# First x halves as two 128-row tiles each, and w1's first slices on another queue, in a SiLU MLP with gradients

## The chip, the cores and the metric

The kernel runs on one core of a Trainium2 chip. The metric is device time in microseconds (us) of one execution; lower is better. Five engines work side by side, each on its own instruction stream: TensorE (PE, with weight loads shown as PEld), VectorE (DVE), ScalarE (ACT), GpSimd (POOL) and SyncE (SP), which here only issues transfers. Transfers issued by SP or ACT wait in that engine's queue and are carried out by DMA engines.

## The reference

A two-layer MLP without bias, and all its gradients. S = 2048 rows, D = 640, F = 1536, everything bf16.

```python
def _fwd_reference(x, w1, w2):
    h = jnp.einsum("bsd,df->bsf", x, w1)
    h = _silu(h)
    out = jnp.einsum("bsf,fd->bsd", h, w2)
    return out

def reference(x, w1, w2, grad_out):
    _out, _vjp = jax.vjp(_f, x, w1, w2)
    _grads = _vjp(grad_out)
    return (_out, *_grads)
```

So there are four outputs: out, and the gradients of x, w1 and w2. In matrix terms: h = x w1, a = silu(h), out = a w2; g = grad_out w2^T, gh = g * silu'(h); gx = gh w1^T, gw1 = x^T gh, gw2 = a^T grad_out.

## The kernel before, in words

The rows are taken in four chunks of SC = 512 (the loop over c, L284). Everything in a chunk is held transposed: features on the 128 partitions, 512 rows along the free axis. D is five blocks of 128 (index dt), F is twelve (index ft), and w1 is loaded in three column thirds of FC = 512 (index fc).

For each chunk there are four matmul stages: h (L206, five matmuls per ft), out (sd_phase, L269, with w2), g (L253) and gx (sd_phase again, with w1T). ScalarE turns h into a (silu_a, L215) and into a tanh (L219); VectorE makes the derivative from it (L221, L222). Two more stages behind the loop compute gw2 (L357) and gw1 (L406, L387) over all rows.

The change is at the very start, before and in the first chunk:

- **Warm matmuls.** L140 to L145: VectorE fills a tile `warm`, and TensorE runs NWARM = 22 matmuls 128x128x128 on it. Nothing reads their result.
- **First loads.** The first chunk's x is not loaded by a transposing transfer, as the later ones are (load_xT, L157), but as it lies in memory, in two halves of 256 rows (load_x_half, L171) into `x_two`. Partition p of a half holds the two adjacent rows 2p and 2p+1, so one partition's data is one run of 2560 bytes. Then come slices of the first column third of w1 (load_w1_rows, L177): row block 0, row block 1, and row blocks 2 to 4. Then the second and third column third (load_w1, L168), w2 (L186), and transposing loads of grad_out, w2 and w1 (L187 to L190). All of these are issued by SP, in this order.
- **Start before the entry wait.** All engines meet at a barrier at the start of the program. The instructions gathered in the list `early` (and whatever precedes them on the same engine) are moved ahead of an engine's wait at that barrier by start_before_entry_wait (L16): the memset, the warm matmuls, both x halves and the first two w1 slices. The third slice and all that follows on SP comes after the wait.
- **ScalarE's first work.** After the barrier: the load of its function table and one activation on a single column (L185), so that the table is there when it is needed.
- **PE transposes.** pe_x_half (L192) takes a half: for each of the five dt, two 128x128 transposes on TensorE (L197, through the identity `ident` that GpSimd makes) into one PSUM tile `tp`, then one copy PSUM to SBUF into `xT` (L199), by VectorE for even dt and ScalarE for odd dt. As a tile holds every second row of the half, the copy writes with a step of two elements (the rearrange "p (s q) -> p q s").
- **First h stage.** h_first (L232) runs the first KM = 2 row blocks dt for the four ft of the first column third in turn (dt outside, ft inside; four PSUM banks open), then for each of these ft the rest of dt, and then ft 4 to 11 whole. So the w1 slices are needed one after the other: block 0 by the first four matmuls, block 1 by the next four, blocks 2 to 4 from the ninth on; the second column third from the twenty-first.

PSUM has eight tiles in the pool ps_h (tag "hp"), shared by the transposes and all matmul groups. What an engine does, and in what order, is the order written in the program after the tile scheduler has arranged it; semaphore waits are added by the framework.

Of the kernel before, what the change touches and what calls it, by code (L numbers as in the profile page):

```python
# [9 lines left out]
ACT = mybir.ActivationFunctionType  # L10
# [5 lines left out]
def start_before_entry_wait(nc, names):  # L16

    def move(nc):
        blocks = nc.m.functions[0].blocks
        entry, home = blocks[0].instructions, blocks[1].instructions
        for engine in {i.engine for i in home if i.name in names}:
            mine = [i for i in home if i.engine == engine]
            last = max(k for k, i in enumerate(mine) if i.name in names)
            moved = mine[: last + 1]
            gate = next(
                k
                for k, i in enumerate(entry)  # L30
                if i.engine == engine and isinstance(i, mybir.InstEventSemaphore)
            )
            taken = {i.name for i in moved}
            for k in reversed(range(len(home))):
                if home[k].name in taken:
                    del home[k]
            for i in reversed(moved):
                entry.insert(gate, i)

    nc.at_finalize(move)  # L40
# [22 lines left out]
def kernel(  # L63
# [11 lines left out]
    nc = tc.nc  # L75
    P = 128
    x2 = x.flatten_outer_dims()
# [5 lines left out]
    S, D = x2.shape  # L83
    F = w1.shape[1]
    ST, DT, FT = S // P, D // P, F // P
    SC = 512
    NCH = S // SC
    STC = SC // P
    FC = 512
# [1 line left out]
    FB = FC // P  # L91
    LAG = 2
    LAG_G = 4
    KM = 2
    NWARM = 22
    dt_in = x.dtype

    dram = ctx.enter_context(tc.tile_pool(name="dram", bufs=1, space=bass.MemoryType.DRAM))
# [13 lines left out]
    w1_v = w1.rearrange("(dt p) f -> p dt f", p=P)  # L112
    w2_v = w2.rearrange("(ft p) d -> p ft d", p=P)
    x_v = x2.rearrange("(st p) d -> p st d", p=P)
# [17 lines left out]
    with ExitStack() as mctx:  # L132
        cpool = mctx.enter_context(tc.tile_pool(name="cpool", bufs=1))
# [6 lines left out]
        warm = cpool.tile([P, P], dt_in, name="warm")  # L140
        early = [nc.vector.memset(warm[:], 1.0)]
        warm_a = cpool.tile([P, 1], FP32, name="warm_a")
        wp = ps_h.tile([P, SC], FP32, name="wp", tag="hp")
        for i in range(NWARM):
            early.append(nc.tensor.matmul(wp[:, 0:P], lhsT=warm[:], rhs=warm[:], start=True, stop=True))  # L145

        ident = cpool.tile([P, P], dt_in, name="ident")
        make_identity(nc, ident[:])

        w1_nat = w1pool.tile([P, DT, F], dt_in, name="w1_nat", tag="w1a")  # L150
# [12 lines left out]
            return goT  # L163

        xT_next = xpool.tile([P, DT, SC], dt_in, name="xT")
        x_two = cpool.tile([P, 2, 2, D], dt_in, name="x_two")

        def load_w1(lo, hi):  # L168
            nc.sync.dma_start(out=w1_nat[:, :, lo:hi], in_=w1_v[:, :, lo:hi])

        def load_x_half(half):  # L171
            lo = half * 2 * P
            return nc.sync.dma_start(
                out=x_two[:, half, :, :], in_=x2[lo:lo + 2 * P, :].rearrange("(p q) d -> p q d", q=2)
            )

        def load_w1_rows(lo, hi):  # L177
            return nc.sync.dma_start(out=w1_nat[:, lo:hi, 0:FC], in_=w1_v[:, lo:hi, 0:FC])

        early += [load_x_half(0), load_x_half(1), load_w1_rows(0, 1), load_w1_rows(1, KM)]  # L180
        load_w1_rows(KM, DT)
        start_before_entry_wait(nc, {i.ins.name for i in early})
        for fc in range(1, NFC):
            load_w1(fc * FC, (fc + 1) * FC)
        nc.scalar.activation(warm_a[:], warm[:, 0:1], ACT.Silu)  # L185
        nc.sync.dma_start(out=w2_nat[:], in_=w2_v[:])  # L186
        goT_next = load_goT(0)  # L187
        for fc in range(NFC):
# [1 line left out]
        nc.sync.dma_start_transpose(out=w1T[:], in_=w1[:, :])  # L190

        def pe_x_half(xT, half):  # L192
            lo = half * 2 * P
            for dt_ in range(DT):
                tp = ps_h.tile([P, 2, P], dt_in, name="tp", tag="hp")
                for q in range(2):
                    nc.tensor.transpose(tp[:, q, :], x_two[:, half, q, dt_ * P:(dt_ + 1) * P], ident[:])  # L197
                copy = nc.scalar.copy if dt_ % 2 else nc.vector.tensor_copy
                copy(out=xT[:, dt_, lo:lo + 2 * P].rearrange("p (s q) -> p q s", q=2), in_=tp[:])  # L199

        pe_x_half(xT_next, 0)
        pe_x_half(xT_next, 1)

        def h_mm(hp, ft, xT, lo, hi):
            for dt_ in range(lo, hi):
                nc.tensor.matmul(  # L206
                    hp[:],
                    lhsT=w1_nat[:, dt_, ft * P:(ft + 1) * P],
                    rhs=xT[:, dt_, :],
                    start=(dt_ == 0),  # L210
                    stop=(dt_ == DT - 1),
                )
# [19 lines left out]
        def h_first(xT, aT, ghT):  # L232
            hps = []
            for ft in range(FB):
                hps.append(ps_h.tile([P, SC], FP32, name="hp"))
            for dt_ in range(KM):
                for ft in range(FB):
                    h_mm(hps[ft], ft, xT, dt_, dt_ + 1)
            for i in range(FT + LAG_G):
                if i < FT:  # L240
                    if i < FB:
                        h_mm(hps[i], i, xT, KM, DT)
                    else:
# [40 lines left out]
        for c in range(NCH):  # L284
            xT, goT = xT_next, goT_next
# [13 lines left out]
            if c == 0:  # L299
                h_first(xT, aT, ghT)  # L300
                nc.sync.dma_start(
                    out=aT_scr[:, c * SC:(c + 1) * SC].rearrange("(ft p) s -> p ft s", p=P), in_=aT[:]
                )
                sd_phase(c, w2_nat, aT, oT_scr)
                for ft in range(FT):
                    g_group(ft, goT, ghT)
                nc.sync.dma_start(
                    out=ghT_scr[:, c * SC:(c + 1) * SC].rearrange("(ft p) s -> p ft s", p=P), in_=ghT[:]
# [4 lines left out]
            for i in range(FT + LAG):  # L313
# [7 lines left out]
                out=aT_scr[:, c * SC:(c + 1) * SC].rearrange("(ft p) s -> p ft s", p=P), in_=aT[:]  # L321
            )
            nc.sync.dma_start(
                out=ghT_scr[:, c * SC:(c + 1) * SC].rearrange("(ft p) s -> p ft s", p=P), in_=ghT[:]
# [7 lines left out]
    with ExitStack() as fctx:  # L332
# [45 lines left out]
        for fc in range(NFC):  # L378
            gh_blk = gh_blks[fc]
            for dt_ in range(DT):  # L380
                if dt_ == DT // 2:
                    store_gw2(fc)
                if fc == NFC - 1 and dt_ == DT - 1:
                    for k, (lo, hi) in enumerate(((0, FC - P), (FC - P, FC))):
# [12 lines left out]
                        else:  # L397
                            nc.vector.tensor_copy(out=g1[:, lo:hi], in_=gp[:, lo:hi])  # L398
                        last_store = nc.sync.dma_start(
                            out=gw1_v[:, dt_, fc * FC + lo:fc * FC + hi], in_=g1[:, lo:hi]  # L400
# [49 lines left out]
```

## Time and profile before

| | us |
|---|---|
| median of 8 runs | 321.0 |
| lowest and highest of these | 320.64, 321.67 |
| the profiled execution: time | 321.24 |
| the profiled execution: span in the profile | 319.5 |
| HBM read and written | 9.83 MB, 28.97 MB |

The profile shows one execution. Its span (319.5) starts with the program's first instruction; the rest of that execution's time (1.74) lies around it. "Busy" of TensorE counts matmuls in flight; since they are pipelined, the distance from start to start tells the rate, and the length of a single one does not. In a timeline, `x20` means that twenty instructions in a row are put in one line, from the first one's start to the last one's end; the brackets tell how long the engine was idle before and what ended that. In the chain that ended last each line is a piece of work that the next one waited for, or followed on its engine. A DMA's issue and its landing are different times: "to landing" is the time from the issue to the last semaphore signal. w1_nat and w2_nat both appear as `w_nat`, since the profile leaves digits out of names.

### The profile page before, as it was taken

What the parts mean: (1) busy time and instruction counts of PE and PEld (TensorE: products, weight loads), DVE (VectorE), ACT (ScalarE), POOL (GpSimd) and SP (SyncE); (2) the same over time, 40 slices, a digit from 0 to 9 for tenths busy, and PEclk for the clock granted to TensorE, in tenths of its full rate; (3) what the DMA queues carried; (4) which work ended last, traced back from release to release, by engine and by line L of the source; (5) the groups of instructions that cost most, each with busy time, mean ns of one, the idle gap of its engine ahead of it and who ended that gap; (6) DMA issues with size and microseconds to landing.
All of it is one profiled execution on the core that took longest, in us unless ns stands there. A gap on an engine that the chain in (4) does not pass through costs nothing.

```text
span 319.5 us, 3570 instructions
## 1 busy us (share of the span) xinstructions
PE 316.2 (99%) x1498; PEld 146.3 (46%) x1498; DVE 102.6 (32%) x182; ACT 77.9 (24%) x142; POOL 0.7 (0%) x6
## 2 busy tenths in 40 slices
PE   9999999999999999999999999999999999999996
PEld 6444444444444444444444444444444444444443
DVE  3771541477510087710147741000000100001001
ACT  4960000545201254411054520110100001001100
POOL 0000000000000000000000000000000000000000
PEclk9999999999999999999999999999999999999999
DMA  8999999999999855292635079809999998995111
GB/s 284 306 197 223 237 307 245 336 261 295 284 275 280 223 187 143 85 309 76 170 109 139 2 258 267 217 23 297 261 215 270 264 261 286 239 292 176 50 37 45
DMA packets 147311, 67.33 MB, mean 211 GB/s; under 512 B 112608, under 2 KB 147040, under 8 KB 147296
## 3 DMA queue, kind: packets, MB, share of 16 engines
q1 hardware_dynamic: 147296, 67.12, 80.9%
q8 instruction: 11, 0.18, 0.2%
q14 instruction: 4, 0.03, 0.0%
HBM read 9.83 MB, written 28.97 MB: 121 GB/s over the span
## 4 chain that ended last, share of the span: by engine, by line
PE 98%; DMA 1%; DVE 0%; issue 0%; DVEq 0%; SPq 0%
PE hp L269 32%; PE hp L206 16%; PE hp L357 16%; PE hp L253 16%; PE hp L406 15%; PE hp L387 1%; DMA x_two<-in_x_dram 1%; PE tp L197 1%; DVE g L398 0%; DVEq L398 0%; SPq L434 0%
## 5 line engine op out<-in xcount | busy, mean ns | idle before, releaser
L206 PE MATMUL hp<-xT,w_nat 128*128 128x512 bf16 x240 | 57.4, 381 | 0.0
L253 PE MATMUL hp<-goT,w2T 128*128 128x512 bf16 x240 | 56.9, 379 | 0.0
L269 PE MATMUL hp<-aT,w_nat 128*128 128x512 bf16 x240 | 52.5, 379 | 0.0
L269 PE MATMUL hp<-ghT,w1T 128*128 128x512 bf16 x240 | 52.5, 379 | 0.0
L357 PE MATMUL hp<-a_blk,go_nat 128*128 128x512 bf16 x240 | 52.0, 379 | 0.0
L406 PE MATMUL hp<-gh_blk,x_nat 128*128 128x512 bf16 x224 | 48.5, 379 | 0.0
L277 ACT ACTIVATE oT<-hp 128x512 bf16<-128x512 f32 x24 | 14.3, 597 | 109.8 <-PE hp L269 109.8
L215 ACT ACTIVATE aT<-hp 128x512 bf16<-128x512 f32 x48 | 29.9, 625 | 33.0 <-PE hp L206 33.0
L206 PEld LDWEIGHTS <-w_nat 128*128 128x128 bf16 x240 | 23.7, 99 | 28.4 <-issue 0.7
L269 PEld LDWEIGHTS <-w1T 128*128 128x128 bf16 x240 | 23.5, 98 | 28.3
L253 PEld LDWEIGHTS <-w2T 128*128 128x128 bf16 x240 | 23.5, 98 | 28.3
L357 PEld LDWEIGHTS <-go_nat 128*128 128x128 bf16 x240 | 23.5, 98 | 28.3
L269 PEld LDWEIGHTS <-w_nat 128*128 128x128 bf16 x240 | 23.4, 97 | 28.4
L279 DVE CAST oT<-hp 128x512 bf16<-128x512 f32 x16 | 11.1, 692 | 76.9 <-PE hp L269 76.9
L260 DVE SCALAR_TENSOR_TENSOR ghT<-ghT,hp 128x512 bf16<-128x512 bf16 x48 | 32.5, 682 | 7.3 <-PE hp L253 7.3
L406 PEld LDWEIGHTS <-x_nat 128*128 128x128 bf16 x224 | 21.9, 98 | 26.4
L222 DVE SCALAR_TENSOR_TENSOR ghT<-aT,v 128x512 bf16<-128x512 bf16 x48 | 32.8, 688 | 0.5
L221 DVE TENSOR_SCALAR v<-t 128x512 bf16<-128x512 f32 x48 | 20.3, 426 | 30.5 <-ACT t L219 30.5
L219 ACT ACTIVATE t<-hp 128x512 f32<-128x512 f32 x48 | 29.8, 625 | 0.0
L417 DVE CAST g<-hp 128x512 bf16<-128x512 f32 x7 | 4.8, 692 | 47.1 <-PE hp L406 27.4
L367 DVE CAST g2T<-hp 128x512 bf16<-128x512 f32 x7 | 4.8, 692 | 46.1 <-PE hp L357 46.1
L365 ACT ACTIVATE g2T<-hp 128x512 bf16<-128x512 f32 x8 | 4.8, 597 | 47.0 <-PE hp L357 47.0
(20 smaller groups left out, 27.0 us busy)
## 6 DMA issues: line engine op xcount, KB each, us to landing
aT_scr<-aT SPq DMA_DIRECT2D x4, 1536.0 KB, 6.2
ghT_scr<-ghT SPq DMA_DIRECT2D x4, 1536.0 KB, 8.0
out_dram<-o_sb SPq DMA_DIRECT2D x8, 640.0 KB, 3.6
oT_scr<-oT SPq DMA_DIRECT2D x4, 640.0 KB, 3.6
go_nat<-in_grad_out_dram SPq DMA_DIRECT2D x4, 640.0 KB, 6.6
x_nat<-in_x_dram SPq DMA_DIRECT2D x4, 640.0 KB, 5.3
gxT_scr<-oT SPq DMA_DIRECT2D x4, 640.0 KB, 4.7
w_nat<-in_w_dram SPq DMA_DIRECT2D x1, 1920.0 KB, 12.9
```

The costliest lines, as they stand in the source:

```text
L206: nc.tensor.matmul(hp[:], lhsT=w1_nat[:, dt_, ft * P:(ft + 1) * P], rhs=xT[:, dt_, :], start=(dt_ == 0), stop=(dt_ == DT - 1),)
L215: nc.scalar.activation(aT[:, ft, :], hp[:], ACT.Silu)
L219: nc.scalar.activation(t[:], hp[:], ACT.Tanh, scale=0.5)
L221: nc.vector.tensor_scalar(out=v[:], in0=t[:], scalar1=-0.5, scalar2=0.5, op0=ALU.mult, op1=ALU.add)
L222: nc.vector.scalar_tensor_tensor(out=ghT[:, ft, :], in0=aT[:, ft, :], scalar=1.0, in1=v[:], op0=ALU.subtract, op1=ALU.mult)
L253: nc.tensor.matmul(gp[:], lhsT=w2T[:, dt_, ft * P:(ft + 1) * P], rhs=goT[:, dt_, :], start=(dt_ == 0), stop=(dt_ == DT - 1),)
L260: nc.vector.scalar_tensor_tensor(out=ghT[:, ft, :], in0=ghT[:, ft, :], scalar=1.0, in1=gp[:], op0=ALU.add, op1=ALU.mult)
L269: nc.tensor.matmul(op_[:], lhsT=w_all[:, ft, dt_ * P:(dt_ + 1) * P], rhs=rhs_all[:, ft, :], start=(ft == 0), stop=(ft == FT - 1),)
L277: nc.scalar.activation(oT[:, dt_, :], op_[:], ACT.Copy)
L279: nc.vector.tensor_copy(out=oT[:, dt_, :], in_=op_[:])
L357: nc.tensor.matmul(gp[:], lhsT=go_nat[:, st, dt_ * P:(dt_ + 1) * P], rhs=a_blk[:, st, :], start=(st == 0), stop=(st == ST - 1),)
L406: nc.tensor.matmul(gp[:], lhsT=x_nat[:, st, dt_ * P:(dt_ + 1) * P], rhs=gh_blk[:, st, :], start=(st == 0), stop=(st == ST - 1),)
```

## The change

Four things are altered, all at the start:

1. x halves: each half is loaded as two tiles of 128 consecutive rows (`x_first`, through the view x_v), so partition p holds rows p and 128 + p of the half, two runs of 1280 bytes. The transposes read these tiles, and the copy writes 256 adjacent elements. KT = DT, so all five column blocks are loaded and copied.
2. w1's three slices are issued by ScalarE instead of SP, and are now row block 0, row block 1, and row blocks 2 to 4, all three in `early`. The activation on `warm_a` stands ahead of them in the text and is, by its place on that engine, moved ahead of the entry wait with them. In the built program ScalarE's order is: slice of block 0, table load, activation, slice of block 1, slice of blocks 2 to 4, entry wait. SP's is: both x halves, entry wait, the second and third column third of w1, w2, and then the transposing loads.
3. KM is 3 instead of 2.
4. NWARM is 23 instead of 22.

Later in SP's order a few transfers change places (for instance the transposing load of the third chunk's x now comes ahead of the first store of oT).

```diff
-    KM = 2
-    NWARM = 22
+    KM = 3
+    NWARM = 23
+    KT = DT
...
-        x_two = cpool.tile([P, 2, 2, D], dt_in, name="x_two")
+        x_first = cpool.tile([P, STC, KT * P], dt_in, name="x_first")
...
         def load_x_half(half):
-            lo = half * 2 * P
-            return nc.sync.dma_start(
-                out=x_two[:, half, :, :], in_=x2[lo:lo + 2 * P, :].rearrange("(p q) d -> p q d", q=2)
-            )
+            rows = slice(2 * half, 2 * half + 2)
+            return nc.sync.dma_start(out=x_first[:, rows, :], in_=x_v[:, rows, 0:KT * P])
 
         def load_w1_rows(lo, hi):
-            return nc.sync.dma_start(out=w1_nat[:, lo:hi, 0:FC], in_=w1_v[:, lo:hi, 0:FC])
-
-        early += [load_x_half(0), load_x_half(1), load_w1_rows(0, 1), load_w1_rows(1, KM)]
-        load_w1_rows(KM, DT)
+            return nc.scalar.dma_start(out=w1_nat[:, lo:hi, 0:FC], in_=w1_v[:, lo:hi, 0:FC])
+
+        early += [load_x_half(0), load_x_half(1)]
+        nc.scalar.activation(warm_a[:], warm[:, 0:1], ACT.Silu)
+        early += [load_w1_rows(0, 1), load_w1_rows(1, 2), load_w1_rows(2, DT)]
         start_before_entry_wait(nc, {i.ins.name for i in early})
         for fc in range(1, NFC):
             load_w1(fc * FC, (fc + 1) * FC)
-        nc.scalar.activation(warm_a[:], warm[:, 0:1], ACT.Silu)
         nc.sync.dma_start(out=w2_nat[:], in_=w2_v[:])
...
         def pe_x_half(xT, half):
-            lo = half * 2 * P
-            for dt_ in range(DT):
+            for dt_ in range(KT):
                 tp = ps_h.tile([P, 2, P], dt_in, name="tp", tag="hp")
                 for q in range(2):
-                    nc.tensor.transpose(tp[:, q, :], x_two[:, half, q, dt_ * P:(dt_ + 1) * P], ident[:])
+                    nc.tensor.transpose(tp[:, q, :], x_first[:, 2 * half + q, dt_ * P:(dt_ + 1) * P], ident[:])
                 copy = nc.scalar.copy if dt_ % 2 else nc.vector.tensor_copy
-                copy(out=xT[:, dt_, lo:lo + 2 * P].rearrange("p (s q) -> p q s", q=2), in_=tp[:])
+                copy(out=xT[:, dt_, half * 2 * P:(half + 1) * 2 * P], in_=tp[:])
```

## The prediction

> **What bounds the kernel now.** I read the busy shares first, then the chain that ended last, then the first 20 us of the timeline, then the DMA issues.
>
> ```profile
> PE 316.2 (99%) x1498; PEld 146.3 (46%) x1498; DVE 102.6 (32%) x182; ACT 77.9 (24%) x142; POOL 0.7 (0%) x6
> ```
>
> TensorE is busy for all but 3.3 us of the span, so only the start and the end can give or cost anything. The chain in order of time (start, length, what):
>
> ```profile
> 0.09 3.05 DMA x_two<-in_x_dram
> 3.18 2.31 PE tp L197 x20
> 5.49 13.42 PE hp L206 x60
> 18.91 12.95 PE hp L269 x60
> ```
>
> The chain is: the first x half lands at 3.14, twenty transposes follow, then sixty h matmuls. Sixty matmuls of the same shape take 13.42 us here and 12.95 in the next stage (0.216 each), so the first sixty lose 0.47 us. The weight loads show where:
>
> ```profile
> 5.18 0.26 PEld L206 LDWEIGHTS <-w_nat 128*128 128x128 bf16 x2
> 5.71 0.15 PEld L206 LDWEIGHTS <-w_nat 128*128 128x128 bf16 x1 [0.28 <-issue]
> 6.14 0.15 PEld L206 LDWEIGHTS <-w_nat 128*128 128x128 bf16 x1 [0.28 <-issue]
> 6.45 2.47 PEld L206 LDWEIGHTS <-w_nat 128*128 128x128 bf16 x12 [0.16 <-issue]
> ```
>
> The first matmuls start at 5.29, 5.71, 6.14 and 6.45: steps of 0.42, 0.43 and 0.31, then 0.216. Nothing is waited for ("issue"): TensorE runs at half rate and changes to full rate inside the third step, at 6.14 + 0.43 x (0.31 - 0.216)/(0.43 - 0.216) = 6.33. The same doubling shows in the 128-column shape:
>
> ```profile
> 0.50 2.53 PE L145 MATMUL wp<-warm 128*128 128x128 bf16 x22 [0.50 <-DVE warm L141]
> 315.80 0.67 PE L387 MATMUL hp<-gh_blk,x_nat 128*128 128x128 bf16 x9
> ```
>
> Less one matmul's own length (0.31 and 0.22), these are 21 steps of 0.106 and 8 of 0.056. The granted clock stands at 1.00 in both windows, so it does not show this. Two consequences: a delay before 6.33 costs half (the work put off is done at twice the rate), a delay behind it costs all.
>
> The data arrive thus (us from issue to landing):
>
> ```profile
> w_nat<-in_w_dram SPq DMA_DIRECT2D x2, 640.0 KB, 7.5
> x_two<-in_x_dram SPq DMA_DIRECT2D x2, 320.0 KB, 3.2
> w_nat<-in_w_dram SPq DMA_DIRECT2D x1, 384.0 KB, 4.2
> w_nat<-in_w_dram SPq DMA_DIRECT2D x2, 128.0 KB, 3.5
> ```
>
> With the issue times on SP's queue (0.09 and 0.54; 1.00, 1.48, 2.05; 2.48) and the single values (3.0 and 3.4 for x; 6.9 for the first 640 KB alone): x half 0 at 3.14, half 1 at 3.97, w1 row block 0 at 4.4, block 1 at 5.1, blocks 2 to 4 at 6.2, the second column third at 9.34. All stand in one queue, in the order in which TensorE reads them.
>
> **The change part by part.**
>
> *Warm matmuls, 22 to 23.* One more step of 0.106 moves their end from 2.82 to 2.93. It lies in the wait for x (until 3.18), which is 0.36 long: nothing. Were x there by 2.93, it would cost up to 0.1.
>
> *Contiguous copies.* Ten copies (DVE 445 ns, ACT 447 ns each) may get shorter. The fourth DVE copy, which the first h matmul needs, runs from 4.81 to 5.24, and the last transpose holds TensorE until 5.29. So they are hidden behind half-rate transposes: nothing. If the rate doubled before the transposes were done, the copy would be last; half of a copy, 0.2 us, bounds the gain.
>
> *KM = 3.* The same 60 matmuls in another order. Bank 0 is complete after 14 instead of 11, so ScalarE's Silu stream starts 3 x 0.216 = 0.65 later. Its last aT now ends at 19.75 (18.95 + 0.80), and its reader is the twelfth matmul of the next stage, 18.75 + 11 x 0.216 = 21.1. The cover is 1.37 us, of which 0.72 is left: nothing. Without cover TensorE would wait for the rest.
>
> *x as two 128-row tiles.* 640 KB now come in runs of 1280 B instead of 2560 B. The bandwidth row of the first 30 us, one figure for each 0.75 us,
>
> ```profile
> GB/s 0 65 280 393 357 257 362 365 369 351 358 355 357 367 361 360 364 367 344 212 42 96 291 301 13 46 279 290 287 111 173 229 290 142 144 211 290 193 108 227
> ```
>
> shows 393 GB/s while the long runs move (its fourth figure) and about 360 while 1 to 1.3 KB runs do: 0.655 MB takes 1.82 instead of 1.67 us, so half 0 is 0.07 and half 1 0.15 later.
>
> *w1's slices on ScalarE's queue.* The changed program's order there is: slice of block 0, table load (1.28), warm activation (0.20), slice of block 1, slice of blocks 2 to 4. ScalarE is ready at 0.14, so with 0.43 per issue they leave at about 0.14, 2.1 and 2.55, done by 2.95; its first copy is at 3.82, so the issuing is hidden (0.87 us of cover). SP loses three issues, and the second and third column thirds of w1 (640 KB each) and w2 leave some 1.4 us sooner, at about 1.0, 1.5 and 2.1. These are now in flight **beside** the slices instead of behind them. Two prices follow.
>
> First, block 0 (131 KB, 0.36 us at 360 GB/s) competes with x. If it goes wholly ahead of the rest of half 0, that lands at 3.57, and the twenty transposes (2.13 at 0.106) end at 5.74, 0.45 late. If it delays half 1 alone, that lands at 4.48, and its ten transposes end at 5.59, 0.30 late; with block 1 ahead as well, 0.66 late. If nothing goes ahead, half 1 at 4.12 is in time for its turn at 4.25: nothing. At half price that is 0 to 0.35; I take 0.2.
>
> Second, blocks 2 to 4 are needed by the ninth h matmul (7.53 now, 7.73 after the first price). Now 1.31 MB have moved when they land at 6.2; when the second column third lands at 9.34, 1.97 MB have. The lower end is 6.2, nothing lost. The upper end is that the whole 640 KB goes ahead: 9.34, 1.6 lost at full price. Equal shares let some 0.34 MB ahead, that is 1.65 MB, by interpolation 7.8. I take 1.75 MB, nearer to equal shares than to the far end: 6.2 + 0.44/0.655 x 3.14 = 8.3, so 0.55 lost. Behind it the ACT stream and everything else are late by the same.
>
> [...] No row here shows two queues at once.
>
> *The other loads.* The second column third has the same 1.97 MB to move up to its end, so it lands as before (9.34, first read at 10.1). w2 lands at 3.58 + 12.9 = 16.5, read at 18.75. A few later stores and transposing loads on SP change places, but from 6.45 on TensorE steps at 0.216 with no wait to the end: nothing.
>
> **Sum.** 0.2 + 0.55 = 0.75. The profiled execution took 321.24, of which the span is 319.5; it would take 321.99. It stands 0.24 above the median of the runs, so against the median of 321.0 the forecast is **321.7 us**, slower by 0.2%.
>
> **Rivals.**
>
> *No late slice (not slower).* The queues share so that blocks 2 to 4 land by 7.7; then only the first price is left, 321.0 + 0.2 = 321.2, or 321.0 if block 0 too goes by unnoticed. For it: 1.5 us of slack now (6.2 against 7.53). Against it: 1.3 MB beside it that used to stand behind it. It turns on the landing of one transfer: at 7.7 it is free, each 0.1 later costs 0.1.
>
> *The rate doubles later.* TensorE's pause before the transposes grows from 0.36 to as much as 0.6 us. If the rise comes a fixed time after the pause (3.15 after 3.18), x's delay costs double, 0.2 more: 321.9. If it makes the whole run-up from 0.50 to 6.33 begin anew at the end of the pause, at about 3.6, full rate comes at 9.4, 3.1 late, at half price 1.5: 323.2 with the first price alone. Against it: the pause of 0.36 did not prevent the rise at 6.33.
>
> [...]
>
> *Faster.* If the rate usually doubles before the transposes end, the shorter copies show (0.2); if x also lands no later and the 0.47 of half-rate loss goes too, 321.0 - 0.2 - 0.47 = 320.3. Against it: the transfers of x got shorter runs and company.
>
> **How the numbers follow.** No change means within 0.2%, 0.64 us: about what runs that spread over 1.03 us can tell. Forecast 0.44, its own range 321.3 to 322.8, of which 0.08 lies within 0.2%; no late slice 0.34, all within; rate later 0.14, slower; faster 0.08. So slower 0.36 + 0.14 = 0.50, same 0.08 + 0.34 = 0.42, faster 0.08. The range for 8 in 10 goes from 320.7, where the first rival and the lowest of the runs shown lie together, to 322.8 (0.2 and the 1.6 of the far end); the last two rivals' far ends are left out.
>
> **What would show it.** The slices of block 1 and of blocks 2 to 4 land after 5.1 and 6.2, and TensorE has a wait on w_nat before the ninth h matmul; x half 1 lands after 4.25 and the transposes end after 5.29; copies under 445 ns without effect. I am wrong if the h matmuls step at 0.216 from the rise on without a gap (then 321.0 to 321.2), or if half-rate steps last beyond 7 us (then above 322).

## The result and the profile after

The changed kernel takes 323.2 us (median of 11 runs, 322.34 to 323.61); the kernel before, timed beside it, 320.8 (31 runs, 320.43 to 322.26). The ratio is 1.0067, 95% interval 1.0057 to 1.0077: slower by 2.2 us (the ratio is of means; the medians differ by 2.4). The forecast was slower, 321.7, with a range up to 322.8; the time lies above the range.

The profiled execution took 323.29 with a span of 320.7, against 319.5 before. The spans of the eleven runs go from 320.3 to 321.7 with a median of 321.2, so this profile shows a quick one. It shows 1.3 us of the loss, all of it in the first 8.2 us: from 7.98 on TensorE works at the same step as before, and the first h stage ends at 20.23 instead of 18.91. The chain that ended last in the kernel after (start, length, what), which answers to the chain shown of before:

```profile
0.08 3.84 DMA x_first<-in_x_dram
...
3.97 1.25 PE tp L195 x10
5.21 0.04 issue
5.26 1.25 PE tp L195 x10
6.50 13.73 PE hp L204 x60
```

The first half of x lands at 3.92 instead of 3.14, the second half makes TensorE wait once more, and the transposes end 1.0 later. The sixty h matmuls take 13.73 where they took 13.42. The weight loads show why:

```profile
3.96 0.98 PEld L195 LDWEIGHTS <-x_first 128*128 128x128 bf16 x10 [1.09 <-DMA x_first<-in_x_dram]
5.25 0.98 PEld L195 LDWEIGHTS <-x_first 128*128 128x128 bf16 x10 [0.31 <-DMA x_first<-in_x_dram]
6.19 0.26 PEld L204 LDWEIGHTS <-w_nat 128*128 128x128 bf16 x2
6.72 0.15 PEld L204 LDWEIGHTS <-w_nat 128*128 128x128 bf16 x1 [0.28 <-issue]
7.15 0.15 PEld L204 LDWEIGHTS <-w_nat 128*128 128x128 bf16 x1 [0.28 <-issue]
7.58 0.15 PEld L204 LDWEIGHTS <-w_nat 128*128 128x128 bf16 x1 [0.28 <-issue]
7.98 2.04 PEld L204 LDWEIGHTS <-w_nat 128*128 128x128 bf16 x10 [0.25 <-issue]
```

The pause before the transposes grew from 0.4 to about 1.1 us, and a second one of 0.3 follows. Four h matmuls (from 6.30, 6.72, 7.15 and 7.58) run at half rate, where it was two and a part. By the prediction's formula the rate doubles at 7.58 + 0.43 x (0.40 - 0.216)/(0.43 - 0.216) = 7.95 instead of 6.33. So x is later and the full rate is later too.

The timeline of ScalarE and its queue, and the DMA issues of the first 30 us, show what x had beside it:

```profile
0.20 0.40 ACTq L177 DMA_DIRECT2D w_nat<-in_w_dram  x1
0.65 1.28 ACT L180 ACT_TABLE_LOAD   x1 [0.65 <-POOLq L432]
0.71 0.88 ACTq L177 DMA_DIRECT2D w_nat<-in_w_dram  x2
...
1.94 0.20 ACT L180 ACTIVATE warm_a<-warm 128x1 f32<-128x1 bf16 x1
```

```profile
x_first<-in_x_dram SPq DMA_DIRECT2D x2, 320.0 KB, 4.2
w_nat<-in_w_dram ACTq DMA_DIRECT2D x1, 384.0 KB, 7.1
w_nat<-in_w_dram ACTq DMA_DIRECT2D x2, 128.0 KB, 3.9
```

The slices did not stay behind the table load. The issuing of the second and third (0.71 to 1.59) runs while the table load (0.65 to 1.93) is under way, though both stand behind the activation in the order. So all three slices leave by 1.6. Block 0 lands at 3.74, x's half 0 at 3.92, block 1 at 5.01, x's half 1 at 5.21. Before, the same 896 KB landed in the order half 0 (3.14), half 1 (3.97), block 0 (4.4), block 1 (5.12). The last of them lands at about the same time; what is needed first now comes last. In the window from 2 to 3 us the two queues (q1 is SP's, q10 ScalarE's; packets, MB, share) are both at work, with 164 and 129 packets:

```profile
q1 hardware_dynamic: 164, 0.20, 56.6%
q10 hardware_dynamic: 129, 0.12, 45.2%
```

### The profile page after: what moved, and what is told of

Read it like the earlier page. It is cut to its first block, busy times and chain, and to the rows that moved or that the text cites. A ratio compares the mean times of both kernels' runs of the same rounds, so it can differ in the third digit from the quotient of the medians.

```text
span 320.7 us, 3578 instructions
## 1 busy us (share of the span) xinstructions
PE 316.7 (99%) x1499; PEld 146.4 (46%) x1499; DVE 101.5 (32%) x182; ACT 77.7 (24%) x142; POOL 0.7 (0%) x6
## 4 chain that ended last, share of the span: by engine, by line
PE 98%; DMA 1%; DVE 0%; issue 0%; DVEq 0%; SPq 0%
PE hp L267 32%; PE hp L204 16%; PE hp L251 16%; PE hp L355 16%; PE hp L404 15%; DMA x_first<-in_x_dram 1%; PE hp L385 1%; PE tp L195 1%; DVE g L396 0%; DVEq L396 0%; SPq L432 0%
```

## The experiments

All were timed in five rounds beside the kernel before. Theory A: w1's slices, in flight beside x, make x late. Theory C: the longer pause of TensorE also puts off the doubling of its rate. Rivals: B, x's shorter runs make it late; D, the pause does not matter.

### One part alone: the layout

```diff
 # the kernel before, with only x_first, its loads and its contiguous copies
-                copy(out=xT[:, dt_, lo:lo + 2 * P].rearrange("p (s q) -> p q s", q=2), in_=tp[:])
+                copy(out=xT[:, dt_, lo:lo + 2 * P], in_=tp[:])
```

> Only x as 128-row tiles with contiguous copies; w1's slices stay on SP behind x, KM and NWARM as before. Theory A (the second queue makes x late): x half 0 lands by 3.4 us and half 1 by 4.3, TensorE's pause before the transposes stays under 0.6 us, time 320.8 to 321.2. Rival B (the short 1280-byte runs make x late): half 0 lands after 3.6 us, time 322 or more.

Measured: 321.07 (before 320.98), ratio 1.0009, interval 0.9995 to 1.0022. Half 0 of x lands at 3.12, half 1 at 4.10. The chain:

```profile
0.08 3.04 DMA x_first<-in_x_dram
...
3.17 2.31 PE tp L195 x20
5.48 13.07 PE hp L204 x60
```

The same 2.31 for twenty transposes without a pause: neither the short runs nor the copies matter by themselves. B falls.

### One part alone: the queue

```diff
 # the kernel before, x in 2560-byte runs; all three slices in `early`, the activation ahead of them as in the change
-            return nc.sync.dma_start(out=w1_nat[:, lo:hi, 0:FC], in_=w1_v[:, lo:hi, 0:FC])
+            return nc.scalar.dma_start(out=w1_nat[:, lo:hi, 0:FC], in_=w1_v[:, lo:hi, 0:FC])
```

> Only w1's slices on ScalarE's queue; x in 2560-byte runs with the strided copies, KM and NWARM as before. Theory A: half 0 of x lands at 3.6 to 3.9 us and half 1 near 5, pause 0.8 to 1.1 us, full rate only after 7 us, time 322.3 to 323.2. Rival B: half 0 by 3.3 us, time 320.8 to 321.2.

Measured: 323.03, ratio 1.0073, interval 1.0046 to 1.01 (six runs, 322.38 to 325.6). The queue alone costs as much as the whole change, within its wide interval. The way there was partly another one: half 0 of x lands at 3.41 and half 1 at 4.57, sooner than expected, and in the profiled execution the rate doubles before the first h matmul. Then the third slice is late. Weight loads of this kernel:

```profile
5.43 1.53 PEld L206 LDWEIGHTS <-w_nat 128*128 128x128 bf16 x8
9.88 1.19 PEld L206 LDWEIGHTS <-w_nat 128*128 128x128 bf16 x7 [2.92 <-DMA w_nat<-in_w_dram]
```

Eight h matmuls run, and the ninth waits for blocks 2 to 4, which land at 9.84 (issue 1.12, 8.7 to landing). It starts 2.6 us later than the step of 0.216 would have it. This is the wait that the prediction's second price is for, and it is beyond that price's upper end (a landing at 9.34, 1.6 lost). With 2560-byte runs x lands 0.5 to 0.65 sooner than in the changed kernel (3.41 against 3.92, 4.57 against 5.21); why was not tried by itself.

### Is it the pause? Filling it, and making one

```diff
 # the changed kernel
-    NWARM = 23
+    NWARM = 33
```

> The changed kernel with 33 instead of 23 warm matmuls, which end at about 4.0 us, when x lands: the pause is filled and no data comes sooner. Theory C (the pause puts off the doubling of TensorE's rate): the h matmuls still start near 6.3 us but at full rate in many executions, time 321.6 to 322.1. Rival D (the pause does not matter, only the late data): 323.2, or up to 0.1 more.

Measured: 321.94 (seven runs, 321.75 to 322.36), ratio 1.0028, interval 1.0014 to 1.0041. Ten more useless matmuls make the changed kernel 1.3 us faster. Its weight loads:

```profile
3.89 0.68 PEld L195 LDWEIGHTS <-x_first 128*128 128x128 bf16 x10
5.04 0.56 PEld L195 LDWEIGHTS <-x_first 128*128 128x128 bf16 x10 [0.47 <-DMA x_first<-in_x_dram]
5.56 1.54 PEld L204 LDWEIGHTS <-w_nat 128*128 128x128 bf16 x8
8.09 2.92 PEld L204 LDWEIGHTS <-w_nat 128*128 128x128 bf16 x15 [0.98 <-DMA w_nat<-in_w_dram]
```

Ten transposes take 0.56 to 0.68 where they took 0.98: the rate doubled as they began, at about 4.0, though x landed late (3.63 and 5.00; that is 0.3 and 0.2 sooner than in the changed kernel's profile, one execution each). Now a new wait shows, the ninth h matmul for blocks 2 to 4, which land at 8.05 (its start comes 0.66 later than the step of 0.216 would have it).

```diff
 # the kernel before
-    NWARM = 22
+    NWARM = 12
```

> The kernel before with 12 instead of 22 warm matmuls: TensorE pauses from 1.8 us until x lands at 3.1; no data is later. Theory C: full rate comes 1 to 3.4 us later than in the kernel before, time 321.8 to 322.6. Rival D: 320.8.

Measured: 322.21, ratio 1.0034, interval 1.0024 to 1.0044. x lands as before (3.2), and its profile has the same half-rate steps as the changed kernel's:

```profile
3.24 2.05 PEld L197 LDWEIGHTS <-x_two 128*128 128x128 bf16 x20 [1.53 <-DMA x_two<-in_x_dram]
5.24 0.26 PEld L206 LDWEIGHTS <-w_nat 128*128 128x128 bf16 x2
5.78 0.15 PEld L206 LDWEIGHTS <-w_nat 128*128 128x128 bf16 x1 [0.28 <-issue]
6.20 0.15 PEld L206 LDWEIGHTS <-w_nat 128*128 128x128 bf16 x1 [0.27 <-issue]
6.63 0.15 PEld L206 LDWEIGHTS <-w_nat 128*128 128x128 bf16 x1 [0.28 <-issue]
7.03 3.98 PEld L206 LDWEIGHTS <-w_nat 128*128 128x128 bf16 x19 [0.25 <-issue]
```

A pause of 1.5 us alone, with no data late, costs 1.2 us between the medians. The profiled execution is a quick one (321.6): by the same formula its full rate comes at 7.00, 0.7 later than before, and the first h stage ends 0.4 later. Both runs agree with C and against D. The edit changes the number of warm matmuls and the pause together; no run parts the two.

### What costs nothing

```diff
 # the kernel before, each alone
-    KM = 2
+    KM = 3
```

> The kernel before with KM = 3 alone. By the prediction's step this is hidden: 320.8, within 0.3. If the later start of the Silu stream (0.65 us) is not hidden, 321.3 to 321.5 and a gap of TensorE at the start of the second stage.

Measured: 320.84, ratio 0.9999, interval 0.9989 to 1.0008: hidden, as worked out. Its profile shows something else. The rate doubles during the transposes (at about 4.4), and TensorE then waits until a strided copy on VectorE has ended at 5.37 (four of these copies stand in the chain that ended last):

```profile
5.42 5.49 PEld L206 LDWEIGHTS <-w_nat 128*128 128x128 bf16 x26 [0.43 <-issue]
```

So the case in which the prediction let the copies count (full rate before the transposes are done) does occur.

```diff
-    NWARM = 22
+    NWARM = 25
```

> The kernel before with 25 instead of 22 warm matmuls, which end at about 3.14, when half 0 of x lands. If even the pause of 0.36 us puts off the full rate in some executions, the slower executions (321.2 and above) get rarer: median 320.7, highest below 321.8. If a pause of that length does not matter: 320.8 to 321.0 with the same spread.

Measured: 320.93, ratio 0.9999, interval 0.9991 to 1.0007. The median did not move. The twelve runs stayed at or below 321.3, while the 35 runs of before reach 321.69; twelve are too few to call that a narrower spread.

### The change without its queue

```diff
 # the changed kernel, the three slices back on SP behind x
-            return nc.scalar.dma_start(out=w1_nat[:, lo:hi, 0:FC], in_=w1_v[:, lo:hi, 0:FC])
+            return nc.sync.dma_start(out=w1_nat[:, lo:hi, 0:FC], in_=w1_v[:, lo:hi, 0:FC])
```

> The changed kernel with w1's three slices back on SP behind x, all else as changed (layout, copies, KM = 3, NWARM = 23). If the queue is the whole cause: 320.8 to 321.2, x half 0 by 3.3 us, pause below 0.4 us. If the other edits cost together: above 321.5.

Measured: 320.91 (before 320.98), ratio 1.0002, interval 0.9991 to 1.0013. Half 0 lands at 3.23, half 1 at 4.14. With one queue undone the whole loss is gone; the other three edits together cost and bring nothing that shows beside an interval of 0.1% to either side. The rate doubles early in this profile (3.57); the h matmuls then wait twice for w1's slices:

```profile
5.82 0.55 PEld L204 LDWEIGHTS <-w_nat 128*128 128x128 bf16 x4 [0.44 <-DMA w_nat<-in_w_dram]
6.90 4.00 PEld L204 LDWEIGHTS <-w_nat 128*128 128x128 bf16 x20 [0.53 <-DMA w_nat<-in_w_dram]
```

### The last wait of the filled kernel

```diff
 # the changed kernel with NWARM = 33
-        early += [load_w1_rows(0, 1), load_w1_rows(1, 2), load_w1_rows(2, DT)]
+        early += [load_w1_rows(0, 1, nc.scalar), load_w1_rows(1, 2, nc.scalar), load_w1_rows(2, DT, nc.sync)]
```

> The changed kernel with 33 warm matmuls and the third slice of w1 (row blocks 2 to 4) on SP ahead of the second column third; the first two slices stay on ScalarE's queue. If in the kernel with 33 warm matmuls alone the wait before the ninth h matmul (0.66 us) is what is left beside the late x, the third slice lands by 7 us, the wait is gone and the time is 321.2 to 321.5. If not: 321.9 as with the slice on ScalarE's queue.

Measured: 321.5 (321.28 to 321.68), ratio 1.0014, interval 1.0006 to 1.0023. The slice lands at 6.36 and the wait is gone. All twelve runs lie below the lowest of the filled kernel (321.75). The weight loads of its h matmuls follow each other without a gap:

```profile
5.97 5.00 PEld L204 LDWEIGHTS <-w_nat 128*128 128x128 bf16 x24
```

The rate doubles at 3.39, among the warm matmuls (their last steps are 0.056), and the last wait is the one for x's half 1 (0.84 by the weight loads). What is left, half a microsecond, goes with the late x (4.00 and 5.41 here).

### The slices really behind the table load: a miss

```diff
 # the changed kernel; the slices overwrite what the activation wrote, and so wait for it
-        nc.scalar.activation(warm_a[:], warm[:, 0:1], ACT.Silu)
+        early.append(nc.scalar.activation(w1_nat[:, :, 0], warm[:, 0:DT], ACT.Silu))
```

> The changed kernel, but the activation writes into w1's tile (a column that the slices then overwrite), so all three slices on ScalarE's queue must wait for the table load and the activation, as the prediction took it. Theory A (what hurts is that the slices leave beside x): they leave from about 1.7 us, half 0 of x lands by 3.4 and half 1 by 4.9, the pause stays under 0.5 us; what is left is the third slice beside the second column third, landing at 7.8 to 8.5, with a wait before the ninth h matmul: 321.3 to 322.0. Rival (any second queue costs the same): 322.8 or more.

Measured: 326.04, ratio 1.0156, interval 1.0143 to 1.0169. Half of the expectation held: x is in time (3.29 and 4.14). But block 0, issued at 1.75, lands only at 8.89, and the first h matmul waits for it:

```profile
8.93 0.13 PEld L204 LDWEIGHTS <-w_nat 128*128 128x128 bf16 x2 [3.55 <-DMA w_nat<-in_w_dram]
```

I had expected the queues to share evenly from the issue on. In the window from 5 to 6 us they did not:

```profile
q1 hardware_dynamic: 292, 0.29, 106.4%
q10 hardware_dynamic: 7, 0.01, 2.0%
```

From 3 to 5 us all 614 packets are SP's. Between 6 and 7 us it is 206 to 112 packets, and from 8 on nearly even (198 to 176 from 8 to 9). So ScalarE's queue got next to nothing for four microseconds after its issue, until the packets of SP's first 640 KB, issued 0.56 us earlier, were almost through. By 7.0 its queue had 119 packets under way, and block 0 is 128 of them; why the last of them landed only at 8.89 the counts do not tell.

```diff
 # the same (NWARM is 23 in both), with the third slice on SP ahead of the second column third
-        early += [load_w1_rows(0, 1), load_w1_rows(1, 2), load_w1_rows(2, DT)]
+        early += [load_w1_rows(0, 1, nc.scalar), load_w1_rows(1, 2, nc.scalar), load_w1_rows(2, DT, nc.sync)]
```

> As the one with all slices behind the table load, and the third slice on SP ahead of the second column third. Theory A: the third slice lands by 7 us, no wait before the ninth h matmul, 320.8 to 321.3. Rival: 322 or more.

Measured: 324.08 (six runs, 322.96 to 325.08), ratio 1.0096, interval 1.0075 to 1.0117. A miss again. The third slice writes the tile that the activation wrote, so on SP, too, it waited for it (issue 1.75); it landed at 8.26, not by 7. Block 0, issued within 0.01 us of it, landed at 6.94, while SP's queue moved 777 packets and ScalarE's 272 (4 to 7 us). The first h matmul waits for it, and after this pause the half rate lasts until about 9.8:

```profile
6.98 0.13 PEld L204 LDWEIGHTS <-w_nat 128*128 128x128 bf16 x2 [1.64 <-DMA w_nat<-in_w_dram]
```

My expectation looked at x and the third slice and forgot that the first slice, too, now had a transfer beside it.

## Why the prediction was wrong

**Bound and place: right.** Only the start mattered. From 7.98 on TensorE works as it did before, 1.3 us later. The direction was right too, but largely by luck: 0.55 of the 0.75 in the sum was for a wait that the changed kernel's profile does not have.

**"Warm matmuls", "Contiguous copies", "KM = 3": right.** Each was costed at nothing; alone (with 25 warm matmuls, and with the copies and the layout in one run) or together they measured 0.9999, 1.0009, 0.9999 and 1.0002. The copies did shrink, from 445 and 447 ns to 292 (VectorE) and 373 (ScalarE), and it changed no median. "x as two 128-row tiles" forecast the halves 0.07 and 0.15 later; alone they landed at 3.12 instead of 3.14 and 4.10 instead of 3.97.

**"w1's slices on ScalarE's queue": the departure times were wrong.** The step has them "leave at about 0.14, 2.1 and 2.55", behind the table load. They left at 0.20, 0.71 and 1.12. So two slices instead of one competed with x.

**The first price: mis-sized, twice.** It put the end of the transposes 0.30 to 0.66 late, and took 0.2 at half price. The profile has the first h matmul 1.0 later (6.30 against 5.29). And half price holds only if the rate doubles at the same moment. It doubled 1.6 later: half-rate steps lasted beyond 7 us, which the prediction had named as a sign that it is wrong ("then above 322"). That was the rival "the rate doubles later", to which I gave 0.14 because a pause of 0.36 had done no harm, and whose far end the range left out. That this far end was 323.2, the time measured, is chance: it had the full rate at 9.4, and it came at 7.95. The run with 33 warm matmuls prices it: 323.2 against 321.94, 1.3 us, more than any other part.

**The second price: the landing was right, its place was not.** Forecast 8.3, measured 8.23. In the changed kernel's profile nobody waits for it: the sum had the ninth h matmul ready at 7.73, and it starts at 8.85. It comes out as soon as the pause is filled (0.66 in that profile; 0.44 between the medians 321.94 and 321.5), and it is the whole wait in the profile with the queue alone. The two are limits of which the later decides. The sum respected that, as it took the second price from 7.73 on; with the first price at its real size, nothing would have been left of the second.

So the loss reads in steps of medians: 323.2; pause filled 321.94; third slice back on SP 321.5; all slices back 320.91. The first is the late rate (1.3), the second the late slice (0.4), the last goes with the late x (0.6; by the ratios 0.4), where the number of warm matmuls goes back from 33 to 23 as well. The two profiles show about 1.3 of the 2.4 between the medians. The rest is probably the spread of the moment at which the rate doubles: the profile of before is one of its slower executions (321.24), that of after one of the shorter spans. With one profiled execution of each, that is not shown.

What the moment of full rate depends on, the runs leave open. The rate doubled 4.0 us after the end of the first pause in the changed kernel (3.97 to 7.95, with a second pause between), and 3.8 us after the pause of 1.5 with 12 warm matmuls (3.24 to 7.00). With 33 warm matmuls and no pause from 0.50 on it doubled at about 4.0, which is 3.5 us after the first matmul; in the run that also has the third slice on SP at 3.39, which is 2.9 us after it. The expectation for 12 warm matmuls had the full rate 1 to 3.4 us later than before; no run shows the 3.4, and that run's profile has 0.7. The granted clock showed 1.00 throughout the profiles of before and after.

## What to carry to other kernels

A second queue is not behind the first: here a transfer that is needed later, put on another queue, took its share from the one that is needed now (x's half 0 at 3.92 instead of 3.14), and what follows on the first queue took its share from the second (blocks 2 to 4 of w1 at 8.23 instead of 6.2). At the start of this kernel ten matmuls that fill a pause on TensorE were worth 1.3 us, more than the late data themselves: count what a pause does to the moment of full rate, not only its own length. Where two late things follow each other on one engine, the later decides, so a price for the second is only as good as the size of the first.

## What the hardware showed that I had not expected

- In the changed kernel ScalarE's queue issued transfers that stand behind a table load and an activation before these were done: issues at 0.71 and 1.12, table load until 1.93, activation at 1.94. What did hold them back was overwriting what the activation had written (issue at 1.75, after the activation, 1.50 to 1.72).
- Two queues shared almost evenly by packets when ScalarE's issue lay 0.07 us ahead of SP's (1.12 and 1.19 in the changed kernel: 326 and 360 packets from 5 to 7 us). When it lay 0.56 us behind, ScalarE's queue got 7 of 299 packets in the window from 5 to 6 us. The gap alone does not decide: in the last run the issues lay within 0.01 us, and ScalarE's queue got 272 of 1049 packets from 4 to 7 us. What decides between the two was not settled.
- In the profiles without a longer pause the moment of full rate lay anywhere from 3.57 us (the change without its queue) to 6.33 (the kernel before). Where it comes early, TensorE is held by something else: in the former by w1's slices (0.44 and 0.53 us by the weight loads), in the one with KM = 3 alone by a copy (0.43). That is a likely reason why faster copies and more warm matmuls bring nothing in the median; it was not tried by itself.
